# Attention with beacon tokens and a SwiGLU block on one core: all large matmuls as pairs of 64-row halves, with PSUM as four slots

## The chip, the cores and the metric

The kernel runs on one core of one Trainium2 chip. The metric is the device time of one execution in microseconds (us), as the median of several runs. Profiles and traces come from one profiled execution.

## What is computed

Eight batches of eight heads, 576 tokens each, 64 values per head. 16 beacon keys and values stand ahead of each head's own ones; every query sees them, and the rest is causal. The attention's output, 4608 tokens of 512 values, goes through a SwiGLU block.

```python
k_all = np.concatenate([beacon_k, k], axis=2)        # 16 + 576 keys
scores = scale * np.matmul(q, k_all.transpose(0, 1, 3, 2))
scores = np.where(causal, -1e9, scores)              # beacons are always seen
a = np.exp(scores - scores.max(-1, keepdims=True))
a /= a.sum(-1, keepdims=True) + 1e-09
x = np.matmul(a, v_all)                              # 8 x 8 x 576 x 64 -> 4608 x 512
g = x @ w_gate                                       # 512 x 1536
out = (g / (1 + np.exp(-g)) * (x @ w_val)) @ w_out   # 1536 x 512
```

All inputs and the output are float32; the kernel computes its matmuls in bf16 and accumulates in float32.

## The kernel before

**Order of the work.** The schedule is written out by hand: a long string, the plan, holds one letter for each piece of work, and `piece` issues the instructions of that letter on their engines. Each engine works through its own instructions in that order and waits where data or a buffer are missing. The letters that matter here: `s`, `d`, `e` are a unit of scores (masked on TensorE, on DVE, on POOL; up to three of them make a burst), `P` is the product of one head's weights with its values (pv), `G` is a unit of gate and value (512 tokens by 128 of the 1536 columns), `F` is one matmul of the output projection, `U` transposes keys and queries of a pair of heads, `X` transposes attention output, `t` is a DMA transpose, `l`, `w`, `o` are loads.

**Attention.** A pair of heads has four units of scores, A to D, with 496, 464, 336+80+80 and 208 query columns. In `scores` (line 291) each matmul contracts the 64 values of one head: the even head of a pair lies on partitions 0 to 63, the odd one on 64 to 127. So the score matmuls use 64 of the array's 128 rows, and the two heads' matmuls follow each other, each into its own PSUM bank. `exponent` (line 261) applies exp on ACT, and masks by POOL (line 269) or DVE (line 265); a few units are masked by a matmul (`mask_on_pe`, line 250). `pv` (line 315) multiplies a head's 128 key rows by 65 columns (64 values and a one, whose product is the softmax's sum), 15 matmuls a head, and DVE normalizes (lines 323, 324).

**Keys and queries.** Those of batch 0 are loaded in runs of six neighbouring rows, regrouped and transposed on TensorE (`transpose_pair`); those of batches 1 and 2 are loaded row by row and transposed on TensorE (`transpose_both`, line 229), those of later batches by DMA (`dma_transposes`). All loads of POOL's queue are issued by POOL and cast to bf16 on the way.

**The block behind.** `gv_mm` (line 360) puts gate and value of a unit into the two banks of one tile: four matmuls with 128 rows and 512 columns for each. `gv_act` takes them through tanh on ACT (line 373) and two DVE operations (lines 375, 378) into `hT`. `out_steps` (line 399) adds twelve matmuls of 128 rows and 512 columns into one bank for 128 tokens; DVE copies the result (line 408) and SP's queue stores it.

**PSUM** has eight banks: three double ones in the pool `big` (scores, gate and value, the transposes of batches 1 and 2), one in `att` (pv) and one in `outp` (projection); small work alternates between the last two (`small`).

Of the kernel before, what the change touches and what calls it, by code (L numbers as in the profile page):

```python
# [14 lines left out]
P = 128  # L15
S = 576
D = 64
# [7 lines left out]

NPE = 3

NPEX = 1

ROWS = 6  # L30
RP = S // ROWS

NHT = 2

NPT = 3

SPLIT = 4

QBLOCKS = [(0, 112), (112, 128), (240, 128), (368, 128), (496, 80)]

# [11 lines left out]
def p_col(t, q):  # L52

    if t == 0 and q >= 496:
        return 1296 + q - 496
    return q + (0, 496 - 112, 960 - 240, 1456 - 368, 1376 - 496)[t]
# [3 lines left out]
def kernel(  # L60
# [21 lines left out]
    NPAIR = H // 2  # L82
    assert NCH == B + 1 and B > NPE
# [8 lines left out]
    big = ctx.enter_context(tc.tile_pool(name="big", bufs=3, space=bass.MemoryType.PSUM))  # L92
    att = ctx.enter_context(tc.tile_pool(name="att", bufs=1, space=bass.MemoryType.PSUM))
    outp = ctx.enter_context(tc.tile_pool(name="outp", bufs=1, space=bass.MemoryType.PSUM))

    ctx.enter_context(tc.manual_schedule())

    ident = static.tile([P, P], BF16, name="ident")
    below = static.tile([P, P], BF16, name="below")
    upper = static.tile([P, P + NB], BF16, name="upper")  # L100


    QK = NKT * H * D
    QKP = ROWS * H * D
    beacons = static.tile([NB, H, D], BF16, name="beacons")
    beacons_in = static.tile([NB, H, D], FP32, name="beacons_in")
    qs = static.tile([P, QKP], BF16, name="qs")
    ks = static.tile([P, QKP], BF16, name="ks")
    first_k = static.tile([RP, 2 * ROWS * D], FP32, name="first_k")
    first_q = static.tile([RP, 2 * ROWS * D], FP32, name="first_q")  # L110
    qb = [static.tile([P, n], BF16, name=f"qb{i}") for i, n in ((0, QKP), (1, QK))]
    kb = [static.tile([P, n], BF16, name=f"kb{i}") for i, n in ((0, QKP), (1, QK))]
# [10 lines left out]
    def tiles(t):  # L123
        return t[:, 0:QK].rearrange("p (c h d) -> p c h d", c=NKT, d=D)

    def load_runs(t, src, h0, h1):
        nc.gpsimd.dma_start(  # L127
            t[0:RP, ROWS * D * h0 : ROWS * D * h1].rearrange("p (h e) -> p h e", e=ROWS * D),
            src[0, h0:h1].rearrange("h (p i) d -> p h (i d)", i=ROWS),
        )  # L130

    heat = []
    loaded = {}

    def rows(eng, dst, src, b, h0, h1, c, p0, r, n):
        key = (b, "v") if src is v or src is beacon_v else (b, src is not q, c)
        loaded[key] = loaded.get(key, 0) + 1
        return eng.dma_start(  # L138
            dst[p0 : p0 + n, c, h0:h1, 0:D], src[b, h0:h1, r : r + n, :].rearrange("h j d -> j h d")
        )  # L140

    def q_loads(b, h0, h1):
        d = tiles(qb[b % 2])
        return [
            lambda c=c, n=n: rows(nc.gpsimd, d, q, b, h0, h1, c, 0, P * c, n)
            for c, n in enumerate((P, P, P, P, 64))
        ]

    def key_loads(eng, d, src, bsrc, b, h0, h1):
        loads = [  # L150
            lambda: rows(eng, d, bsrc, b, h0, h1, 0, 0, 0, NB),
            lambda: rows(eng, d, src, b, h0, h1, 0, NB, 0, P - NB),
        ]
        for c, n in ((1, P), (2, P), (3, P), (4, 80)):
            loads.append(lambda c=c, n=n: rows(eng, d, src, b, h0, h1, c, 0, P * c - NB, n))
        return loads

    def k_loads(b, h0, h1):
        return key_loads(nc.gpsimd, tiles(kb[b % 2]), k, beacon_k, b, h0, h1)

    def v_loads(b, h0, h1):
        return key_loads(nc.gpsimd, vb[b % 2], v, beacon_v, b, h0, h1)
# [10 lines left out]
    def load_wo(i):  # L173
        fs = slice(6 * i, 6 * i + 6)
        nc.gpsimd.dma_start(  # L175
            wo[:, fs, :], moe_w_out.rearrange("(f p) e -> p f e", p=P)[:, fs, :]
        )


    def parts_of(eng):  # L180
        return ((nc.vector, 0, SPLIT), (nc.scalar, SPLIT, ROWS)) if eng is None else ((eng, 0, ROWS),)

    def regroup(dst, src, m, eng):
        cols = slice(2 * ROWS * D * m, 2 * ROWS * D * (m + 1))
        to = dst[0:RP, cols].rearrange("p (i h d) -> p i h d", i=ROWS, h=2)
        of = src[0:RP, cols].rearrange("p (h i d) -> p i h d", i=ROWS, h=2)
        for e, i0, i1 in parts_of(eng):
            copy(e, to[:, i0:i1], of[:, i0:i1])
# [7 lines left out]
    def transpose_pair(dst, src, n, m, pool, tag, eng):  # L196
        t_ps = pool.tile([P, KPAD], BF16, name="t_ps", tag=tag)
        h = slice(2 * m, 2 * m + 2)

        first = n - 64  # L200
        if first:
            nc.tensor.transpose(t_ps[:, 0:NB], beacons[:, h, :], ident[0:NB, 0:NB])
        for i in range(ROWS):
            col = P * (ROWS * m + i)
            nc.tensor.transpose(
                t_ps[:, NB + RP * i : NB + RP * i + RP], src[0][0:RP, col : col + P], ident[0:RP, 0:RP]
            )
        if first:
            copy(eng or nc.vector, dst[0][:, m, 0:NB], t_ps[:, 0:NB])
        to = dst[0][:, m, first : first + S].rearrange("q (p i) -> q p i", i=ROWS)  # L210
        of = t_ps[:, NB : NB + S].rearrange("q (i p) -> q p i", i=ROWS)
        for e, i0, i1 in parts_of(eng):
            copy(e, to[:, :, i0:i1], of[:, :, i0:i1])

    def transpose_k(m, pool, tag, eng=None):
        transpose_pair(kT, kb, 80, m, pool, tag, eng)

    def transpose_q(m, pool, tag, eng=None):
        transpose_pair(qT, qb, 64, m, pool, tag, eng)

    def transpose_both(b, m, engines):

        t_ps = big.tile([P, 2, 1024], BF16, name="t2_ps", tag="big")
        h = slice(2 * m, 2 * m + 2)
        for i, src in ((0, kb), (1, qb)):
            t = tiles(src[b % 2])
            for c in range(NKT):
                r = P if c < 4 else 80 if src is kb else 64
                nc.tensor.transpose(t_ps[:, i, P * c : P * c + r], t[0:r, c, h, :], ident[0:r, 0:r])  # L229
        for i, dst, n, eng in ((0, kT, NB + S, engines[0]), (1, qT, S, engines[1])):  # L230
            copy(eng, dst[b % 2][:, m, 0:n], t_ps[:, i, 0:n])

    def dma_transposes(b):
        def one(dst, src, c, n):
            assert loaded[b, src is kb, c] == (2 if src is kb and c == 0 else 1)
            nc.sync.dma_start_transpose(
                dst[b % 2][:, :, P * c : P * c + n],
                src[b % 2][0:n, H * D * c : H * D * c + H * D],
            )

        todo = []
        for c in range(NKT):
            todo.append(lambda c=c: one(kT, kb, c, P if c < 4 else 80))
            todo.append(lambda c=c: one(qT, qb, c, P if c < 4 else 64))
        return todo

    def mask_on_pe(u, ps):
        for hh in range(2):
            for col, n, d in UNITS[u][3]:
                nc.tensor.matmul(  # L250
                    ps[:, hh, col : col + n],
                    lhsT=below[:],
                    rhs=ident[:, d : d + n],
                    start=False,
                    stop=(col, n, d) == UNITS[u][3][-1],
                )

    def exponent(b, m, u, mask, ps):
        c0, w, _, diagonals = UNITS[u]
        p = pt[(NPAIR * b + m) % NPT]  # L260
        nc.scalar.activation(p[:, :, c0 : c0 + w], ps[:, :, 0:w], ACT.Exp, scale=0.125)  # L261
        for col, n, d in [] if mask == "s" else diagonals:
            ap = p[:, :, c0 + col : c0 + col + n]
            if mask == "d":
                nc.vector.tensor_tensor(  # L265
                    out=ap, in0=ap, in1=upper[:, None, d : d + n].to_broadcast([P, 2, n]), op=ALU.mult
                )
                continue
            nc.gpsimd.affine_select(  # L269
                out=ap,  # L270
                in_=ap,
                compare_op=ALU.is_ge,
                fill=0.0,
                base=d,
                pattern=[[0, 2], [1, n]],
                channel_multiplier=-1,
            )

    def scores(burst):

        tiles = [big.tile([P, 2, 512], FP32, name="s_ps", tag="big") for _ in burst]
        while heat:
            heat.pop()
            nc.tensor.matmul(
                tiles[0][:, 0, 0 : 2 * P], lhsT=pt[2][:, 0, 0:P], rhs=pt[2][:, 0, 0 : 2 * P], start=True, stop=True
            )
        for (b, m, u, mask), ps in zip(burst, tiles):
# [10 lines left out]
            if mask != "s":  # L298
                exponent(b, m, u, mask, ps)
# [193 lines left out]

# [162 lines left out]
```

The softmax here doesn't subtract the row's maximum and nothing guards it: scores larger than these inputs give would overflow.

## Time and profile before

| | |
|---|---|
| time, three runs | 370.61 us (median), 370.41 to 372.05 |
| profiled execution, first to last instruction (span) | 370.0 us |
| what lies around the span, median less span | 0.6 us |
| TensorE, VectorE (DVE), ScalarE (ACT), GpSimd (POOL) busy | 98%, 66%, 46%, 39% |
| granted TensorE clock, mean | 0.999 |
| DMA packets | 160,978, of which 149,040 under 512 bytes |

How to read the lines: a group's line gives the source line, the engine, the operation with what it writes and reads, the array's rows*columns, the shape and the count; behind the bar stand the time covered, the mean ns of one, and the idle time before them with what ended it. Matmuls are pipelined, so one begins before the one ahead has ended; where they follow each other closely, the distance of their starts is their price, not their duration. PE is TensorE's matmuls, PEld its weight loads. The timeline's rows give start, duration, and how many equal instructions are merged into the row.

### The profile page before, as it was taken

What the parts mean: (1) busy time and instruction counts of PE and PEld (TensorE: products, weight loads), DVE (VectorE), ACT (ScalarE), POOL (GpSimd) and SP (SyncE); (2) the same over time, 40 slices, a digit from 0 to 9 for tenths busy, and PEclk for the clock granted to TensorE, in tenths of its full rate; (3) what the DMA queues carried; (4) which work ended last, traced back from release to release, by engine and by line L of the source; (5) the groups of instructions that cost most, each with busy time, mean ns of one, the idle gap of its engine ahead of it and who ended that gap; (6) DMA issues with size and microseconds to landing.
All of it is one profiled execution on the core that took longest, in us unless ns stands there. A gap on an engine that the chain in (4) does not pass through costs nothing.

```text
span 370.0 us, 7297 instructions
## 1 busy us (share of the span) xinstructions
PE 360.8 (98%) x2851; PEld 179.3 (48%) x2851; DVE 242.8 (66%) x485; ACT 170.8 (46%) x246; POOL 143.7 (39%) x235
## 2 busy tenths in 40 slices
PE   7898989999999999999999999999999999999996
PEld 3653455655445555444455454544554444444443
DVE  4848767768827677576666765758476856655652
ACT  5933376853482567464554356254642312212110
POOL 8975569696199563726236014030200000000000
PEclk9999999999999999999999999999999999999999
DMA  9999999999999999989939859455102100001013
GB/s 165 139 191 179 191 166 149 137 168 140 173 113 197 130 135 140 166 112 112 185 54 108 77 114 86 67 61 98 59 31 41 51 30 28 30 29 57 2 59 111
DMA packets 160978, 39.61 MB, mean 107 GB/s; under 512 B 149040, under 2 KB 156464, under 8 KB 160944
## 3 DMA queue, kind: packets, MB, share of 16 engines
q0 software_dynamic: 112304, 18.83, 72.0%
q1 hardware_dynamic: 48432, 20.02, 27.7%
q8 instruction: 22, 0.36, 0.4%
q10 hardware_dynamic: 208, 0.29, 0.3%
q14 instruction: 12, 0.10, 0.1%
HBM read 38.27 MB, written 9.44 MB: 129 GB/s over the span
## 4 chain that ended last, share of the span: by engine, by line
PE 84%; POOL 7%; DMA 7%; DVE 1%; issue 1%; ACT 0%; POOLq 0%
PE gv_ps L360 45%; PE o_ps L399 25%; PE pv_ps L315 7%; PE s_ps L291 6%; DMA kb<-in_k_dram 3%; DMA vb<-in_v_dram 3%; POOL vb L138 2%; POOL kb L138 1%; PE t_ps L229 1%; POOL wg L167 1%; POOL p L269 1%; PE o_ps L419 1%; POOL wv L167 1%; POOL wo L175 0%; POOL qs L127 0%
## 5 line engine op out<-in xcount | busy, mean ns | idle before, releaser
L373 ACT ACTIVATE th<-gv_ps 128x512 f32<-128x512 f32 x108 | 64.4, 597 | 157.7 <-PE gv_ps L360 152.6
L375 DVE SCALAR_TENSOR_TENSOR u<-th,gv_ps 128x512 f32<-128x512 f32 x108 | 74.2, 687 | 63.5 <-ACT th L373 62.2
L360 PE MATMUL gv_ps<-xT,wg 128*128 128x512 bf16 x432 | 111.8, 379 | 1.3 <-DVE hT L378 1.3
L360 PE MATMUL gv_ps<-xT,wv 128*128 128x512 bf16 x432 | 111.8, 379 | 0.2 <-DMA wv<-in_moe_w_val_dram 0.2
L261 ACT ACTIVATE p<-s_ps 128x992 bf16<-128x992 f32 (+2 forms) x128 | 101.6, 869 | 21.8 <-PE s_ps L291 19.5
L399 PE MATMUL o_ps<-wo,hT 128*128 128x512 bf16 x420 | 110.1, 380 | 0.1
L378 DVE SCALAR_TENSOR_TENSOR hT<-gv_ps,u 128x512 bf16<-128x512 f32 x108 | 74.7, 691 | 3.7
L269 POOL TENSOR_SCALAR_AFFINE_SELECT p<-p 128x256 bf16<-128x256 bf16 (+2 forms) x86 | 32.8, 407 | 111.0 <-ACT p L261 108.4
L360 PEld LDWEIGHTS <-wv 128*128 128x128 bf16 x432 | 42.2, 98 | 51.3 <-DMA wv<-in_moe_w_val_dram 0.7
L360 PEld LDWEIGHTS <-wg 128*128 128x128 bf16 x432 | 41.0, 98 | 47.3 <-issue 1.5
L399 PEld LDWEIGHTS <-hT 128*128 128x128 bf16 x420 | 36.9, 98 | 42.4 <-issue 5.9
L315 PEld LDWEIGHTS <-p 128*128 128x128 bf16 x960 | 36.5, 97 | 14.6 <-issue 2.7
L315 PE MATMUL pv_ps<-vb,p 128*128 128x65 bf16 x960 | 40.1, 193 | 1.3 <-DMA vb<-in_v_dram 0.9
L265 DVE TENSOR_TENSOR p<-p,upper 128x256 bf16<-128x256 bf16 (+2 forms) x60 | 16.6, 300 | 29.2 <-ACT p L261 28.9
L138 POOL DMA_DIRECT2D vb<-in_v_dram x40 | 34.1, 865 | 3.7 <-DMA kb<-in_k_dram 2.3
L291 PE MATMUL s_ps<-qT,kT 64*128 64x80 bf16 (+4 forms) x384 | 33.1, 281 | 0.8 <-ACT p L261 0.7
L138 POOL DMA_DIRECT2D qb<-in_q_dram x35 | 30.4, 869 | 7.1 <-DVE p L265 3.1
L324 DVE TENSOR_TENSOR x<-pv_ps,rec 128x320 bf16<-128x320 f32 x64 | 31.5, 492 | 2.3
L138 POOL DMA_DIRECT2D kb<-in_k_dram x35 | 30.5, 871 | 3.4 <-DMA wo<-in_moe_w_out_dram 3.1
L408 DVE COPY o_sb<-o_ps 128x512 f32<-128x512 f32 x35 | 23.9, 684 | 7.3 <-PE o_ps L399 7.2
L291 PEld LDWEIGHTS <-kT 64*128 64x128 bf16 x384 | 13.8, 94 | 21.0 <-issue 16.3
L323 DVE RECIPROCAL rec<-pv_ps 128x5 f32<-128x5 f32 x64 | 12.0, 188 | 11.2 <-PE pv_ps L315 10.9
(57 smaller groups left out, 83.8 us busy)
## 6 DMA issues: line engine op xcount, KB each, us to landing
out_dram<-o_sb SPq DMA_DIRECT2D x35, 256.0 KB, 2.3
qb<-in_q_dram POOLq DMA_DIRECT2D x28, 128.0 KB, 6.5
vb<-in_v_dram POOLq DMA_DIRECT2D x24, 128.0 KB, 5.4
kb<-in_k_dram POOLq DMA_DIRECT2D x21, 128.0 KB, 6.6
wg<-in_moe_w_gate_dram POOLq DMA_DIRECT2D x4, 384.0 KB, 9.8
wv<-in_moe_w_val_dram POOLq DMA_DIRECT2D x4, 384.0 KB, 8.7
wo<-in_moe_w_out_dram POOLq DMA_DIRECT2D x2, 768.0 KB, 11.0
vb<-in_v_dram POOLq DMA_DIRECT2D x8, 112.0 KB, 4.8
```

Of the source, the lines that this page charges most:

```text
L138: return eng.dma_start(dst[p0 : p0 + n, c, h0:h1, 0:D], src[b, h0:h1, r : r + n, :].rearrange("h j d -> j h d"))
L261: nc.scalar.activation(p[:, :, c0 : c0 + w], ps[:, :, 0:w], ACT.Exp, scale=0.125)
L269: nc.gpsimd.affine_select(out=ap, in_=ap, compare_op=ALU.is_ge, fill=0.0, base=d, pattern=[[0, 2], [1, n]], channel_multiplier=-1,)
L291: nc.tensor.matmul(ps[:, hh, col : col + n], lhsT=kT[b % 2][r, m, P * t : P * t + P], rhs=qT[b % 2][r, m, q0 : q0 + n], start=mask != "s" ...
L315: nc.tensor.matmul(o_ps[:, c, 0 : D + 1], lhsT=pt[(NPAIR * b + m) % NPT][:, hh, col : col + P], rhs=vb[b % 2][:, t, h, 0 : D + 1], start=( ...
L324: nc.vector.tensor_tensor(out=xs[b][:, :, D * h : D * h + D], in0=o_ps[:, :, 0:D], in1=rec[:].to_broadcast([P, NKT, D]), op=ALU.mult,)
L360: nc.tensor.matmul(gvs[f][:, TOK * half : TOK * half + TOK], lhsT=w[:, kk, P * f : P * f + P], rhs=xT[:, kk, r : r + TOK], start=(kk == 0) ...
L373: nc.scalar.activation(th[:], ps[:, 0:TOK], ACT.Tanh, scale=0.5)
L375: nc.vector.scalar_tensor_tensor(out=u[:], in0=th[:], scalar=1.0, in1=ps[:, 0:TOK], op0=ALU.add, op1=ALU.mult)
L378: nc.vector.scalar_tensor_tensor(out=hTs[j][:, f, :], in0=ps[:, TOK:1024], scalar=0.5, in1=u[:], op0=ALU.mult, op1=ALU.mult)
L399: nc.tensor.matmul(st["o"][:], lhsT=hTs[j][:, f, P * i : P * i + P], rhs=wo[:, f, :], start=(f == 0), stop=(f == NF - 1),)
L408: nc.vector.tensor_copy(o_sb[:], st["o"][:])
```

## The change

Every large matmul is cut along its contraction into two halves of 64 rows. One half contracts partitions 0 to 63, the other 64 to 127, and the two of a pair write two banks of one PSUM tile. In the first phase the lower half works on the first bank's sum (gate, or the first 128 tokens, or the first head) while the upper half works on the second bank's (value, the next 128 tokens, the second head). In the second phase they swap, so that each bank gets the other 64 rows. Between the phases of one tile, `halves` issues a nop on TensorE that waits for the last matmul of that tile's first phase. Transposes of keys and queries and the masks on TensorE are in 64-row halves too; the transposes of attention output in batch 0 (`x_turn`) stay at 128 rows.

All PSUM work takes one of four double banks (`take`, `give`), the one that has been free longest by the work list's order. pv and its normalization take two heads at once, the projection two blocks of 128 tokens. Keys and queries of batches 0 to 2 are loaded in runs of nine rows (keys on the lower 64 partitions, queries on the upper) and regrouped and turned on TensorE; so there are 118 loads in place of 135, and the weights stand earlier in POOL's queue. Exp, masks, tanh and the DVE steps have letters of their own in the work list, 23 of the output copies are on DVE and 15 on ACT, and 79 masks are on DVE and 67 on POOL.

The diff, cut to its core:

```diff
-NPEX = 1
-ROWS = 6
+HALF = 64
+ROWS = S // HALF
+NSLOT = 4
...
+    def take(key, shape, dtype, name):
+        i = spare.pop(0)
+        held[key] = i
+        t = slots[i].tile(shape, dtype, name=name, tag="slot")
+        for bank in range(2):
+            writers.pop((i, bank), None)
+        return t
+
+    def give(key):
+        spare.append(held.pop(key))
+
+    def halves(key, bank, row, o, l, r, start, stop, turn=False):
+        at = (held[key], bank)
+        was = writers.get(at)
+        if was is not None and was[0] != row:
+            last = max((w for (i, _), w in writers.items() if i == at[0]), key=lambda w: w[2])
+            if last[3]:
+                gate = nc.tensor.nop()
+                tc.add_manual_dep(
+                    gate.ins,
+                    last[1],
+                    mybir.DependencyInfo(mybir.DependencyClass.Sync, mybir.DependencyReason.DATA),
+                    reason="one bank, two row halves",
+                )
+            for other, w in writers.items():
+                if other[0] == at[0]:
+                    writers[other] = (w[0], w[1], w[2], False)
...
+            ins = nc.tensor.matmul(o, lhsT=l, rhs=r, start=start, stop=stop)
+        order[0] += 1
+        writers[at] = (row, ins.ins.name, order[0], True)
...
+    def turn(n):
...
+        for i in range(ROWS):
+            for row in range(2):
+                r = slice(HALF * row, HALF * row + HALF)
+                halves(("t", n), row, row, t_ps[:, row, HALF * i : HALF * i + HALF], g[r, i, :], ident[r, r], 1, 1, True)
...
+    def pv(n, second):
+        b, m = divmod(n, NPAIR)
+        if not second:
+            pvs[n] = take(("p", n), [P, 2, 512], FP32, "pv_ps")
+        o_ps = pvs[n]
         for c, (q0, _) in enumerate(QBLOCKS):
             for t in range(c + 1):
                 col = p_col(t, q0)
...
+                for row in (1, 0) if second else (0, 1):
+                    hh = row ^ second
+                    r = slice(HALF * row, HALF * row + HALF)
+                    halves(
+                        ("p", n), hh, row, o_ps[:, hh, 68 * c : 68 * c + D + 1],
+                        pt[n % NPT][r, hh, col : col + P], vb[b % 2][r, t, 2 * m + hh, 0 : D + 1],
+                        c == 0 and t == 0 and not second, second and c == t == NKT - 1,
+                    )
...
+        for second, kk in steps:
+            for row in (1, 0) if second else (0, 1):
+                half = row ^ second
+                k64 = slice(HALF * row, HALF * row + HALF)
+                halves(
+                    ("g", n), half, row, ps[:, half, :],
+                    (wg, wv)[half][k64, kk, P * f : P * f + P], xT[k64, kk, r : r + TOK],
+                    half not in seen, final and (second, kk) == steps[-1],
                 )
...
+            second, f = divmod(st, NF)
+            for row in (1, 0) if second else (0, 1):
+                bank = row ^ second
+                k64 = slice(HALF * row, HALF * row + HALF)
+                halves(
+                    key, bank, row, projected[pr, part][:, bank, cols],
+                    hTs[j][k64, f, P * (i + bank) : P * (i + bank) + P], wo[k64, f, cols],
+                    st == 0, st == 2 * NF - 1,
                 )
...
+        elif kind == "G":
+            gate_value(n + wholes, [(0, kk) for kk in range(KD)], False)
+        elif kind == "H":
+            gate_value(n + wholes, [(1, kk) for kk in range(KD)], True)
...
+        "2Ha1Ga2G1H2Ga1H2Ga1H2Ha1FaFFF2FFG12GHHa1Ga2FFF1G2FFFHGa1H2Ha1Ga2FFF1G2FFFFFFFFFFoFFFoFFFFFFFFHHa",
```

In the new work list `S` or `s` is a unit of scores, `E` its exp, `D` or `M` its masks, `P` and `p` are the two phases of pv, `R` the normalization, `G` and `H` the two phases of gate and value, `a`, `1`, `2` the steps from them to `hT`, `F` one pair of the projection, `O` and `o` the output copies, `T` a turn of keys and queries.

## The prediction

> **What bounds the kernel now.** The page comes first: its busy shares, and the chain that ended last.
>
> ```profile
> PE 360.8 (98%) x2851; PEld 179.3 (48%) x2851; DVE 242.8 (66%) x485; ACT 170.8 (46%) x246; POOL 143.7 (39%) x235
> ...
> PE 84%; POOL 7%; DMA 7%; DVE 1%; issue 1%; ACT 0%; POOLq 0%
> ```
>
> TensorE has work all the time, and no other engine is near it; the 14% of POOL and DMA in the chain lie before 53 us. A busy TensorE may still be held up, so I asked the groups by shape and then the timeline of one stretch.
>
> ```profile
> L360 PE MATMUL gv_ps<-xT,wv 128*128 128x512 bf16 x432 | 111.8, 379 | 0.2 <-DMA wv<-in_moe_w_val_dram 0.2
> L399 PE MATMUL o_ps<-wo,hT 128*128 128x512 bf16 x420 | 110.1, 380 | 0.1
> L315 PE MATMUL pv_ps<-vb,p 128*128 128x65 bf16 x960 | 40.1, 193 | 1.3 <-DMA vb<-in_v_dram 0.9 <-DVE x L324 0.2
> L291 PE MATMUL s_ps<-qT,kT 64*128 64x496 bf16 x64 | 12.1, 374 | 0.1
> ```
>
> A matmul of 512 columns shows 379 ns from first to last, but they start 216 ns apart. The 64 score matmuls of 496 columns cover 12.1 us, which is 32 times 378 ns: the two halves (rows 0 to 63, rows 64 to 127) of a pair run at once.
>
> ```profile
> 160.17 1.03 PE L360 MATMUL gv_ps<-xT,wv 128*128 128x512 bf16 x4
> 161.13 0.58 PE L291 MATMUL s_ps<-qT,kT 64*128 64x496 bf16 x4
> 161.64 0.82 PE L399 MATMUL o_ps<-wo,hT 128*128 128x512 bf16 x3
> 162.30 0.62 PE L315 MATMUL pv_ps<-vb,p 128*128 128x65 bf16 x15
> 162.76 0.81 PE L399 MATMUL o_ps<-wo,hT 128*128 128x512 bf16 x3
> 163.50 0.69 PE L291 MATMUL s_ps<-qT,kT 64*128 64x336 bf16 x10
> 164.12 0.39 PE L399 MATMUL o_ps<-wo,hT 128*128 128x512 bf16 x1
> ```
>
> Each row's start plus its matmuls times their pitch should be the next row's start. 160.17 + 4 x 0.216 = 161.03, but the scores start at 161.13. Their pairs of 496 and 464 columns stream 0.40 us, to 161.53, but the projection starts at 161.64. 162.30 to 162.76 is 15 x 0.030, with nothing lost. So about 0.1 us goes wherever 128-row and 64-row work meet, and nowhere else. Taking every start in the trace less columns/2.4 + 2.5 ns: 115 such meetings lose 95.7 ns each (11.0 us), 6 around the 16-row beacon transposes lose 0.65 us, and the first matmul or pair behind a meeting takes 10 ns more (226 instead of 216), 1.15 us: 12.8 us in all.
>
> ```profile
> PEld L291 <- issue: 16.3, 39, 0.6
> ...
> PE gv_ps L360 <- DVE hT L378: 1.3, 1, 1.3
> ...
> PE pv_ps L315 <- DMA vb<-in_v_dram: 0.9, 2, 0.5
> PE s_ps L291 <- ACT p L261: 0.7, 2, 0.4
> ```
>
> The waits say the same: weights for scores stand idle at 39 places for nothing the profile shows. Real waits behind the first transpose add up to 7.1 us, all but 0.2 before 61 us.
>
> The sum of the span of 370.0 us: first real matmul 6.0; streaming 341.2 (gate and value 186.5, projection 93.2, pv 28.4, scores with masks 26.0, transposes 7.2); meetings and their followers 12.2 (net of some 0.6 where pairs start early); waits 7.1; tail 3.3. The three runs have a median of 370.6, so 0.6 lies around the span.
>
> **The change, part by part.**
>
> *Every large matmul as two 64-row halves: -11.9 us.* With all work in 64-row halves the meetings go: -12.8. The four transposes of x in batch 0 (x_turn) stay at 128 rows, 8 meetings x 0.106 = +0.85. Price of a pair: in the scores, behind the first pair of a burst, pairs follow each other after columns/2.4 + 2 to 3 ns (80 to 80 columns, 31 of 31; 336 to 80, 16 of 16), the next weights loading 8 to 10 ns after the current pair starts. 512/2.4 + 2.5 = 216, what a 128-row matmul takes now. So 1296 pairs of the MLP cost the same: 0, with a bound of +10 ns each (the first pair's excess), +13.0.
>
> The Trainium skill speaks against this: "TensorE: Matmul & The Clock Gate", section "Wait — 56ns, not 53.3ns?", has matmuls start at least 25 ns apart however small. By that figure a pv pair would take 50 ns instead of 29, an estimate of +20 us over 960 pairs, and the gain would be gone. The trace's halves start 3 to 4 ns apart, so I go by the trace.
>
> *pv: +1.5 us (0 to +9.3).* The 960 matmuls of 128x65 become 960 pairs for two heads at once. Nearest rows: 29 ns for one of 65 columns, 35 for a pair of 80. New is the number of instructions, four in 29 ns. From an empty queue (a semaphore instruction at 221.73) to the next such one at 222.16, TensorE's sequencer passed 40 instructions in 0.387 us, 9.7 ns each; by that a pair takes 39 ns, 10 x 960 = 9.3 us if the sequencer never runs ahead. The trace has it up to 33 instructions ahead, over half of one phase's 60. I take 1.5.
>
> *The swap: +3.0 us (2.7 to 4.6).* Between a slot's first and second phase `halves` puts a nop that waits for the slot's last matmul; behind it queues all further TensorE work, and through it the exp, tanh and copies. From the end of streaming: 379 - 216 = 163 ns until the matmul ends, 14 to the semaphore's event, 43 to a start (the medians of TensorE's waits); or, where a sequencer instruction (51 ns) waits, 57 more behind it: 230 to 330 ns. I went through the new work list and added up the streaming between each slot's last first-phase matmul and its gate: of 162 gates, 112 have over 450 ns, 33 have 250 to 450 (mostly 425 to 444, two projection steps), 7 have 89 to 214 and 10 have none (five in the first 13 us of this streaming, two by 41, three in the last projections). 10 x 0.23 to 0.33, 7 x about 0.06 to 0.16 and a few tens of ns for six of 254 to 311: 2.7 to 4.6; part of the early ones lie under waits for data.
>
> *Keys and queries of batches 1 and 2 by runs: -2.7 us on TensorE.* 132 transposes (6.2 us) become 12 turns of 9 pairs of 64 columns, 29 ns each, and 12 for beacons: 3.5. If the pairs ran one half after the other it would be 6.7, +0.5. Beside it, off the path: 22 row loads on POOL (0.55 to 0.87 us each) become 5 loads at 0.65 to 0.74, so POOL's queue gets some 15 us shorter; eight more regroupings on DVE, 8 x 0.75 (the 96x768 copy at 0.50, times 1.5) = 6 us; the copies to kT and qT stay near 0.53 to 0.74 each. DVE's normalization falls from 64 x 0.68 to 32 x at most 1.17 us. DVE keeps about a third idle, so this is nothing; without that cover the 6 us would be the price.
>
> *Masks on TensorE: -0.6 us.* 28 matmuls of 80 to 128 columns (1.4 us) become 28 pairs of up to 64 (0.8). POOL's masks fall from 86 to 67, DVE's rise from 60 to 79, 19 x 0.3 = 5.7 us under DVE's idle time. Exp and tanh are unchanged; 15 output copies move to ACT, 15 x 0.6 = 9 us, into its 54% of idle time.
>
> *Four slots and the new order: +1.0 us (-3 to +6).* pv and the projection each had a bank of their own; now each takes one of four two-bank slots, which leaves two or three for scores or gate and value. The late MLP stage fits: a gate-value unit holds a slot for 1.73 us of matmuls and 0.60 + 0.69 + 0.69 + some 0.1 of ACT and DVE, 3.8 us in all; three slots would turn one over every 1.3 us, and TensorE needs 1.73. In the attention stage two slots for scores turn over in 0.2 + 1.0 (exp) each. Weights come earlier and batch 1's keys cost fewer packets, so the early waits of 7.1 may shrink by 3 or, the order being new, grow; I leave them and put 1.0 for slots.
>
> Sum: 370.0 - 11.9 - 2.7 - 0.6 + 1.5 + 3.0 + 1.0 = 360.3, and 0.6 around it: 360.9 us.
>
> **The rivals.**
>
> *Slots run short (slower).* With the projection and pv each holding a slot, a score unit must wait for an exp to release one. Place: each of the 32 pairs of heads, from 50 to 280 us. Price: one exp (1.0 us) less the first pv phase (0.45) that covers it, 0.55 x 32 = 17.6: 378 us. It cancels the gain from 0.30 us a pair on and makes it slower from 0.36. For it: scores now wait only 0.7 us in all because three double banks serve them. Against: ACT is 46% busy, and a burst's exp has other work behind it.
>
> *Pairs and instructions cost their upper bounds in part.* Half of pv's 9.3 and 3 ns on each of 1296 pairs: 4.7 + 3.9 - 1.5 = +7.1: 368 us. For it: instructions on TensorE nearly double, and every gate takes away the sequencer's lead. Against: the 31 of 31.
>
> *The meetings don't go; a swap is one.* Swapping halves drains the array as a change of shape does: 162 x 0.106 = 17.2: 378 us. Against: halves alternate in the scores at 3 ns with no loss; only accumulation into one bank from both halves is new.
>
> **How the numbers follow.** Forecast 0.68, with its own range 355 to 366 (upper: gates 4.6, pv 5, slots 2; lower: waits 3 less, pv and slots 0). Slots 0.15, upper bounds 0.13, swap as a meeting 0.04. About 0.5% (1.9 us) can be told from no change. Faster: 0.68 + 0.08 of the second rival = 0.76; same: 0.04 of it and 0.02 of the first = 0.06; slower: 0.13 + 0.01 + 0.04 = 0.18. The range 355 to 373 leaves out 0.06 below and some 0.14 above.
>
> **What would show it.** Right: gate and value matmuls in two halves 3 to 4 ns apart, pairs at 216 ns; no 0.1 us between scores and their neighbours; pv pairs at 29 to 35 ns; TensorE starts at most 0.33 us late at a swap, and only where nothing lies between. Wrong: pairs at 226 or more, pv pairs near 39 or 58, waits of scores for an exp of several us in all, or waits behind 61 us.

## The result and the profile after

After: 425.87 us (median, 424.41 to 429.09); before, on the same chip: 370.83 us (370.41 to 372.05). The ratio is 1.149 (95% interval 1.143 to 1.154): 15% slower, where 360.9 us with a range of 355 to 373 had been predicted. The profiled execution of after has a span of 424.1 us. Further down, runs over 1.5% above the fastest of their kernel (two of one_gate's four, one of filled's six) are left out of times and ratios as slow.

The page of after first: shares of the span, granted clock in 40 slices, a queue of instruction fetches (number, MB, share of the DMA engines), and the chain that ended last.

```profile
PE 391.4 (92%) x5263; PEld 186.5 (44%) x5263; DVE 233.6 (55%) x424; ACT 184.6 (44%) x266; POOL 123.0 (29%) x200
PEclk9777959999999999999999999999999999999999
q8 instruction: 41, 0.67, 0.7%
PE 83%; DMA 9%; POOL 3%; issue 2%; ACT 1%; DVE 0%; ACTq 0%
```

TensorE fell from 98% to 92% busy although its busy time grew by 30.6 us: it is held up in the middle of its work. The granted clock shows sevens and a five in the first 64 us, where it was at half for 27 us. No other engine came nearer to the bound. TensorE's timeline shows one unit of gate and value (start, duration, instructions):

```profile
355.28 0.38 PE L132 MATMUL gv_ps<-xT,wv 64*128 64x512 bf16 x1
355.49 0.38 PE L132 MATMUL gv_ps<-xT,wg 64*128 64x512 bf16 x1
355.50 0.38 PE L132 MATMUL gv_ps<-xT,wv 64*128 64x512 bf16 x1
355.71 0.38 PE L132 MATMUL gv_ps<-xT,wg 64*128 64x512 bf16 x2
356.16 0.39 PE L132 MATMUL gv_ps<-xT,wv 64*128 64x512 bf16 x1
356.17 0.39 PE L132 MATMUL gv_ps<-xT,wg 64*128 64x512 bf16 x1
356.39 0.38 PE L132 MATMUL gv_ps<-xT,wv 64*128 64x512 bf16 x1
```

Until 355.71 a pair starts every 0.216 us, its halves some 4 ns apart, as predicted. One of the two `wg` at 355.71 opens a unit's second phase, behind the gate; it starts 3 ns after its neighbour, so this gate cost nothing. The `wv` that should come with it or 0.216 us later starts at 356.16: for 0.45 us no matmul starts. The waits of the weight loads show how often (total, times, longest):

```profile
PEld L132 <- PE gv_ps L132: 63.4, 121, 0.6
PEld L132 <- PE o_ps L132: 10.5, 25, 0.6
PEld L132 <- POOL p L329: 10.2, 2, 9.8
PEld L132 <- PE pv_ps L132: 9.3, 28, 0.6
```

TensorE waits for itself 174 times: about the 162 swaps, not the ten at which nothing lies between. (Weight loads run ahead, so these times overlap the matmuls; the standstills of the array itself are shorter, see the table.) The third row is nearly all one wait of 9.8 us for a mask of POOL.

To see the parts, I let every matmul stream its columns at the granted clock from its recorded start and sorted what is left of each span: *work* (streaming at full clock), standstills of the array by length, *one half* (one half of the rows streaming alone, half of that time), *clock* (lost to half clock, that is a granted clock of 0.5; ahead of the clock's first record the first matmuls start 0.427 us apart, so half clock is taken there). In us:

| kernel | span | work | 60-150 ns | 150-350 ns | over 700 ns | other idle | one half | clock |
|---|---|---|---|---|---|---|---|---|
| before | 370.0 | 335.4 | 12.4 | 1.9 | 6.9 | 11.3 | 0.7 | 1.5 |
| after | 424.1 | 331.4 | 1.3 | 42.1 | 19.4 | 5.0 | 15.6 | 9.2 |
| masks_only | 415.2 | 331.4 | 1.6 | 41.8 | 9.1 | 5.2 | 16.1 | 10.0 |
| one_gate | 392.4 | 331.4 | 1.8 | 3.5 | 34.6 | 3.9 | 7.5 | 9.7 |
| one_gate_masks | 390.6 | 331.4 | 1.3 | 4.1 | 32.2 | 4.3 | 7.5 | 9.8 |
| data_on_time | 373.3 | 331.4 | 1.5 | 3.5 | 15.8 | 5.3 | 7.2 | 8.6 |
| pv_whole | 375.7 | 331.4 | 12.3 | 3.0 | 11.0 | 7.8 | 4.6 | 5.6 |
| filled | 371.2 | 331.4 | 1.3 | 4.4 | 14.1 | 6.9 | 6.6 | 6.5 |

The meetings (60 to 150 ns) went, as they should: 12.4 to 1.3. In their place came 178 standstills of 0.24 us, longer waits, and half clock.

### The profile page after: what moved, and what is told of

The parts are those of the page before. It is cut to its first block, busy times and chain, and to the rows that moved or that the text cites. A ratio compares the mean times of both kernels' runs of the same rounds, so it can differ in the third digit from the quotient of the medians.

```text
span 424.1 us, 12037 instructions
## 1 busy us (share of the span) xinstructions
PE 391.4 (92%) x5263; PEld 186.5 (44%) x5263; DVE 233.6 (55%) x424; ACT 184.6 (44%) x266; POOL 123.0 (29%) x200
## 4 chain that ended last, share of the span: by engine, by line
PE 83%; DMA 9%; POOL 3%; issue 2%; ACT 1%; DVE 0%; ACTq 0%
PE gv_ps L132 47%; PE o_ps L132 24%; PE pv_ps L132 8%; DMA qk<-in_q_dram 4%; PE s_ps L132 4%; DMA wv<-in_moe_w_val_dram 4%; DMA first<-in_k_dram 1%; POOL p L329 1%; ACT p L316 1%; POOL qk L169 1%; POOL qk L160 0%; PE t_ps L130 0%; POOL wg L200 0%; POOL wv L200 0%; POOL wo L208 0%
## 5 line engine op out<-in xcount | busy, mean ns | idle before, releaser
L132 PE MATMUL gv_ps<-xT,wg 64*128 64x512 bf16 x864 | 218.1, 381 | 0.6 <-ACT p L316 0.2
L132 PE MATMUL gv_ps<-xT,wv 64*128 64x512 bf16 x864 | 200.8, 381 | 8.2
L132 PE MATMUL o_ps<-wo,hT 64*128 64x512 bf16 (+2 forms) x912 | 126.4, 365 | 1.5
L132 PEld LDWEIGHTS <-wv 64*128 64x128 bf16 x864 | 67.3, 94 | 87.8 <-PE gv_ps L132 58.1
L132 PEld LDWEIGHTS <-wg 64*128 64x128 bf16 x864 | 68.7, 94 | 48.5 <-PE gv_ps L132 3.0
L132 PEld LDWEIGHTS <-hT 64*128 64x128 bf16 x912 | 49.9, 94 | 41.9 <-PE o_ps L132 10.2
L132 PE MATMUL pv_ps<-vb,p 64*128 64x65 bf16 x1920 | 50.1, 192 | 13.9 <-POOL p L329 9.9
L132 PEld LDWEIGHTS <-p 64*128 64x128 bf16 x1920 | 40.0, 95 | 29.9 <-POOL p L329 10.2
L361 DVE TENSOR_TENSOR x<-pv_ps,rec 128x640 bf16<-128x640 f32 x32 | 26.4, 824 | 1.2
L169 POOL DMA_DIRECT2D qk<-in_q_dram x25 | 21.5, 860 | 12.0 <-DMA qT<-qk 9.4
## 6 DMA issues: line engine op xcount, KB each, us to landing
wv<-in_moe_w_val_dram POOLq DMA_DIRECT2D x4, 384.0 KB, 10.8
wo<-in_moe_w_out_dram POOLq DMA_DIRECT2D x2, 768.0 KB, 12.4
```

The source lines that it names most:

```text
L132: ins = nc.tensor.matmul(o, lhsT=l, rhs=r, start=start, stop=stop)
L169: return nc.gpsimd.dma_start(dst[p0 : p0 + n, c, :, 0:D], src[b, :, r : r + n, :].rearrange("h j d -> j h d"))
L361: nc.vector.tensor_tensor(out=xs[b][:, :, P * m : P * m + P].rearrange("p c (h d) -> p h c d", d=D), in0=o[:, :, :, 0:D], in1=rec[:].to_br ...
```

## The experiments

**The theory.** Reading `halves` again after the result: the gate sets the flags of a slot to False, but the matmul behind it records itself with True. The next matmul, on the other bank and the other rows, finds the slot's latest writer to be *that* matmul, flagged True, and issues a second gate, which waits for the matmul just issued. Nothing can lie between. So the theory (A) is a second gate at each of 162 swaps. Its rivals: swapping halves costs this by itself (B), or the gate that is left is hidden only in part (C).

**one_gate: the second gate taken out.** It asks whether the entry that the new matmul replaces was still ungated; the first gate already waits for every matmul of the first phase.

```diff
-            if last[3]:
+            if was[3]:
```

> Only the second gate of each swap is taken away (the one that waits for the swap's own first matmul). Theory A: that second gate is what costs; 162 swaps lose 0.234 us of standstill, 0.010 for the pair behind it and about 0.1 for the half that streams alone, 55 us together; a span of about 369 us against 424. Rival B: the swap itself drains the array, whatever the number of gates, since the first gate stays: over 415 us. Rival C: the single gate is hidden only in part (0.1 us each): about 385.

Measured: 396.5 us (two runs, 394.1 and 398.9), ratio 1.069 (1.061 to 1.077). TensorE's waits for itself, 174 in after, are down to 15:

```profile
PEld L132 <- PE gv_ps L132: 3.8, 8, 1.0
PEld L132 <- PE o_ps L132: 2.1, 5, 0.6
PEld L132 <- PE pv_ps L132: 0.3, 2, 0.2
```

The standstills of 150 to 350 ns fell from 42.1 to 3.5 us and *one half* from 15.6 to 7.5: 46.7 us, or 0.29 us a swap, so A holds, and B and C fall: 3.5 us is close to the 1.9 of before. But the time fell by 29 us (the span by 31.7) and not by the 55 forecast: standstills over 0.7 us grew from 19.4 to 34.6. The gates had hidden other waits, which none of the three names.

**drain_before: the price of such a gate, in the kernel before.** Each of the 108 gate-and-value units gets one nop behind its first value matmul, waiting for it.

```diff
+                if half == 1 and kk == 0:
+                    gate = nc.tensor.nop()
+                    tc.add_manual_dep(gate.ins, mm.ins.name, ...)
```

> The kernel before, with one nop in each of its 108 gate-value units that waits for the matmul just issued, as the second gate of a swap does. Theory A: each lets the array stand 0.234 us and delays the next matmul by 0.010: 108 x 0.244 = 26 us more, 397. Rival: without halves the queue hides part of it: under 385.

Measured: 395.99 us, ratio 1.067 (1.063 to 1.071); (396.0 - 371.1) / 108 = 0.23 us each. The waits show them, all but one:

```profile
PEld L360 <- PE gv_ps L360: 58.8, 107, 0.6
```

The price is the same with 128 rows as with the 64 of after (0.24 us). After's 0.29 has also the half that streams alone.

**masks_only and one_gate_masks: the long wait for POOL.** POOL's timeline in after (start, duration, instruction, idle before and what ended it):

```profile
47.03 0.89 POOL L169 DMA_DIRECT2D vb<-in_v_dram  x1 [2.63 <-PE s_ps L132]
51.95 0.73 POOL L169 DMA_DIRECT2D vb<-in_v_dram  x1 [4.04 <-DMA wo<-in_moe_w_out_dram]
54.47 0.53 POOL L169 DMA_DIRECT2D qk<-in_beacon_k_dram  x1 [1.78 <-DMA qk<-in_k_dram]
57.53 0.83 POOL L169 DMA_DIRECT2D qk<-in_k_dram  x1 [2.54 <-DMA qk<-in_q_dram]
...
60.11 1.06 POOL L329 TENSOR_SCALAR_AFFINE_SELECT p<-p 128x256 bf16<-128x256 bf16 x3
```

Loads of later batches wait for earlier transfers (4.04, 1.78, 2.54 us); masks that pv needs from 50.8 us on stand behind them in POOL's order and run at 60.11. The two kernels give the masks of six units (the forecasts say five) to DVE (`M` to `D` in the work list), one with both gates, one with the first alone.

> Both gates of each swap stay; only the masks of five units of batch 1 move from POOL to DVE. If the standstill at 51 us is POOL's queue: 414 us, 10 less than 424. If it is the data: 424.

> The same with the masks of five units of batch 1 moved from POOL to DVE, so that pv no longer waits behind POOL's loads. Theory A and the 9.8 us standstill before pv at 51 us as a cost of its own: about 360 us, near the forecast. Rival: something else (a load, exp) keeps that pv waiting, so no more than 2 us below the kernel with one gate alone.

Measured: masks_only 416.76 us (1.124; 1.121 to 1.127), one_gate_masks 392.24 us (1.056; 1.050 to 1.063). With both gates the long wait goes and the time falls by 9, about as expected. With one gate it falls by 4 (the span by 1.8), to 392 and not to the 360 forecast: a wait for masks stays. Taking the second gate out is worth 24.5 us here (416.76 - 392.24), as against 29 without the masks moved; 46.3 us of standstills and half-empty array go, and 23.1 us come back in standstills over 0.7 us. The waits of one_gate_masks name them:

```profile
PE gv_ps L132 <- DMA xT<-x: 7.3, 3, 3.5
PE pv_ps L132 <- POOL p L329: 7.2, 1, 7.2
PE pv_ps L132 <- issue: 5.0, 4, 1.8
PE gv_ps L132 <- issue: 1.8, 1, 1.8
```

One more mask behind loads; three waits for the DMA transposes of attention output into `xT`, which a slower TensorE had hidden; and pauses in which TensorE waited for nothing that the profile shows, as in this piece of the chain of one_gate_masks:

```profile
115.49 0.39 PE pv_ps L132 x26
115.87 1.76 issue
117.63 0.24 PE pv_ps L132 x4
```

A fetch of 16 KB of instructions begins at 114.94 in the trace, 2.7 us before TensorE goes on. Five such pauses (7.7 us) end 2.4 to 3.0 us after the start of a fetch; the kernel before has none, with 22 fetches against 41. After and masks_only, which are slower, have the same 41 and no such pause behind the first 30 us.

**whole_mlp: 64-row halves for attention alone.** One_gate_masks with gate, value and projection at 128 rows.

```diff
-            for row in (1, 0) if second else (0, 1):
-                halves(("g", n), half, row, ps[:, half, :], (wg, wv)[half][k64, ...], xT[k64, ...], ...)
+            nc.tensor.matmul(ps[:, second, :], lhsT=(wg, wv)[second][:, ...], rhs=xT[:, ...], ...)
```

> One gate and moved masks as before, and the MLP's matmuls whole again (128 rows, gate's four and then value's four in the same places of the work list); scores, pv and turns stay in halves. By the price of a meeting of 64- and 128-row work (0.106 us), the work list has 283 of them instead of 8: 275 x 0.106 = 29 us more than with halves, less up to 3 us of gates of the MLP: about 387 us. If halves cost the MLP anything per pair, less than that.

Measured: 405.15 us, ratio 1.092 (1.089 to 1.096); 13 us above one_gate_masks, not 27. The meetings are priced right: 245 standstills of 60 to 150 ns make 24.7 us, 0.101 each. What I missed is on the other side: with 31 fetches instead of 41 the pauses fall from 6.8 us in TensorE's waits to 1.2, all in the first 30 us, and the waits for `xT` from 7.3 to 3.1. The rest of the 14 us was not taken apart.

**data_on_time: masks and transposes in time.** One gate, the masks of positions 150 to 330 of the work list on DVE, and `V`, which issues the DMA transposes of a batch's attention output, directly behind the batch's last `R`.

```diff
-        "Gal1SGEl2SHlEDPaDSHE1p2aMSRGE1MH2SGaE1SHME2PaDSFpE1FFRFSFEFF2SFFFEDMFFDFcPcTcpkTQFFkFQTFFqRSFFEF",
+        "Gal1SGEl2SHlEDPaDSHE1p2aDSRGE1DH2SGaE1SHDE2PaDSFpE1FFRFSFEFF2SFFFEDDFFDFcPcTcpkTQFFkFQTFFqRVSFFE",
```

> One gate; all POOL masks up to the end of batch 1's attention on DVE; the DMA transposes of attention output issued directly behind the normalization of each batch's last heads instead of up to 22 pieces later. If pv's wait for POOL (7.3 us) and the three waits of gate and value for those transposes (7.8 us) are delays of their own: 375 us, and with the half clock that follows such a standstill 371. Rival: the waits for transposes were pauses for instructions in disguise, which stay: 383.

Measured: 375.04 us, ratio 1.011 (1.005 to 1.016), as expected for the waits; the 371 that counted on half clock going too was not reached. What still stands against it are these waits, and half clock (8.6 against 1.5 us):

```profile
PE pv_ps L132 <- issue: 4.0, 4, 1.8
PE gv_ps L132 <- DMA xT<-x: 3.4, 1, 3.4
```

**pv_whole: fewer instructions, with the meetings.** data_on_time with pv at 128 rows (a `for hh` matmul in place of the two `halves`).

> The same, with pv as whole matmuls of 128 rows, one head in each of the two places, so 1,920 fewer instructions on TensorE. If the pauses behind instruction fetches (7.7 us) come from too many short instructions in a row: they vanish, and 126 meetings of 64- and 128-row work at 0.106 us add 12.5: about 5 us more than the kernel it is made from. If those pauses are something else, they stay, and it is 12 us more.

Measured: 377.68 us, ratio 1.018 (1.014 to 1.022), 2.6 above data_on_time. 126 standstills of 60 to 150 ns make 12.3 us, 10.8 more, but after the start no pause behind a fetch is left and half clock lost 3.0 less. That the fetches *cause* the pauses is not shown; fewer instructions took them away in both kernels that had fewer.

**column_halves_before: instructions by themselves.** The kernel before, each MLP matmul as two of 256 columns.

```diff
+                for c in (0, TOK // 2):
+                        gvs[f][:, TOK * half + c : TOK * half + c + TOK // 2],
```

> The kernel before, with every matmul of the MLP as two of 256 columns behind two weight loads, all 128 rows: 2,568 more instructions on TensorE, no swap, no gate, no new work list. If the mere number of instructions at 54 ns each is free: 1,284 more starts at 2.5 ns, 3.2 us more, 373.6. If instructions run short at that number: over 380.

Measured: 374.2 us, ratio 1.008 (1.006 to 1.011): 1284 more matmuls cost 3.1 us, 2.4 ns each. Number alone, at 108 ns each, is nearly free; of the five pauses of one_gate_masks four came where instructions are shortest, in pv, and one in gate and value.

**filled, warm_start, filled_and_warm: the half clock and the last wait.** data_on_time, with twelve `F` moved ahead of the wait of 3.4 us; with 21 pieces (the forecasts say 18) of two dummy matmuls where TensorE waits for loads at the start; with both.

> Kernel: data_on_time with the twelve projection steps of batch 1 moved in front of chunk 4's first gate-and-value matmuls, and nothing else. Theory: the xT wait at 179.6 (3.58 us) falls below 1 us and no half clock follows it (182.4 to 189.2 before, 3.4 us lost): 375 - 2.6 to 3.6 - 3.4 = 368 to 369. Rival (half clock not tied to the standstill): 371 to 372, with an interval of half clock still somewhere behind 170 us. If the next chunk's transfer only comes later by as much, nothing changes: 375.

> Kernel: data_on_time with 18 pieces of two 64-row matmuls of 256 columns, whose products nobody reads, in places of the first 10 us where TensorE waits for loads, and nothing else. Theory: the half clock of 8.3 to 18.5, which follows TensorE's idle time at the start, goes; it lost up to 5 us, and some of TensorE's work there waits for loads anyway: 370 to 372. Rival (half clock at the start belongs to something other than TensorE's idle time, or waits for loads hide it): 374 to 376, and the extra matmuls cost at most 1 us.

> Kernel: data_on_time (373.3 us of span) with two edits. (1) Twelve projection steps of batch 1 are moved in the work list to just before the first gate-and-value matmuls of chunk 4, where TensorE stood 3.58 us for chunk 4's xT at 179.6. (2) 18 pieces of two 64-row matmuls of 256 columns, whose products nobody reads, are put into places of the first 10 us where TensorE waits for loads. Theory (standstills of about 2 us and more cost twice: the wait itself, and some 3.4 to 10 us of half clock behind it): the wait of 3.58 goes and with it the half clock of 182.4 to 189.2 (3.4 us lost), and the half clock of 8.3 to 18.5 (up to 5 us lost) goes too: 373.3 - 2.6 to 3.6 - 3.4 - 4 to 5 = 361 to 364 of span, 363 to 366 with what lies around it, below the kernel before (371). Rival (the half clock has its own rhythm, or the pauses behind instruction fetches move with the work and open it elsewhere): only the wait goes, 369 to 372, the same as before.

Measured: 374.13 (1.008; 1.005 to 1.010), 380.08 (1.025; 1.023 to 1.027) and 378.44 us (1.019; 1.016 to 1.023). The wait for `xT` fell from 3.4 to 1.5 us in filled, and the half clock at 182.4 to 189.2 went; but an interval of half clock came at 24.7 and a new pause of 1.0 us behind a fetch at 154, and the median moved by less than the runs' spread, not to the 368 to 369 forecast. In warm_start the half clock at 8.3 to 18.5 went, as forecast, and the kernel became 5 us slower: the dummy matmuls stream for 2.4 us, score matmuls there wait for exp (0.61 us at 14.8, 0.46 at 15.7), another interval of half clock came at 28.8, and later waits for `xT` grew to 6.2 us. My forecast of 4 to 5 us gained by a warm start was wrong, and with it the 363 to 366 of both edits; what bounds that stage was not taken apart. No version beat the kernel before.

**long_stands and short_stands: what half clock follows.** The kernel before, with six standstills of 2.74 us, or 24 of 0.92, set into gate-and-value units: a nop that waits for four additional tanh, or one.

```diff
+                    if stood[0] in (48, 58, 68, 78, 88, 98):
+                        for _ in range(4):
+                            act = nc.scalar.activation(stand[:], gvs[f][:, 0:TOK], ACT.Tanh, scale=0.5)
+                        gate = nc.tensor.nop()
+                        tc.add_manual_dep(gate.ins, act.ins.name, ...)
```

> Kernel: the kernel before, with six standstills of TensorE set in by hand in the gate-and-value units 48, 58, 68, 78, 88 and 98 of 108: behind the first value matmul a nop waits for four additional tanh (0.60 us each) into a tile that nobody reads, so TensorE stands for about 2.6 us each time, 15 to 16 us in all. Theory (a standstill of 2 us and more is followed by half clock): the profile shows intervals of half clock behind them, 3.4 us or more each, which cost another 1.7 us or more: 371 + 15.6 + 10 or more = 396 or more. Rival (half clock has its own rhythm and only met the standstills by chance): granted clock stays at 1.0 as in the kernel before, 386 to 388.

> Kernel: the kernel before, with 24 short standstills in every second gate-and-value unit from 48 to 94: the nop waits for one additional tanh, so TensorE stands for about 0.8 us, 19 us in all. Theory (the half clock follows the length of one standstill, not their sum): no half clock, granted clock 1.0, 371 + 19 = 388 to 391. Rival (it follows the idle share): half clock here too, 395 or more.

Measured: 391.77 us (1.058; 1.054 to 1.062) and 392.74 us (1.062; 1.057 to 1.066). The granted clock of long_stands, then of short_stands:

```profile
PEclk9999999999999999998999999999998998999999
```

```profile
PEclk9999999999999999999999999999999999999999
```

Three of the six long standstills are followed by 3.4 us of half clock (from 181.8, 294.5 and 321.8 us; the standstills end at 181.6, 294.4 and 320.8), three by none; none of the short ones is. 6 x 2.74 + 3 x 1.7 = 21.5, measured 21.1; 24 x 0.92 = 22.1, measured 22.0. So half clock does follow single long standstills, but not each, and not the sum of idle time. In one_gate it followed one of 2.1 us (ended at 123.2, half clock from 123.8); two of 1.9 to 2.0 us in one_gate_masks were followed by none. My forecast for long_stands took it for each and was 4 us too high. The Trainium skill ("TensorE: Matmul & The Clock Gate", section "HAM oscillation — how this bites in real kernels") warns of idle gaps over about 3.4 us; here 2.74 us were enough in half of the cases.

## Why the prediction was wrong

**The step that failed: "The swap: +3.0 us (2.7 to 4.6)".** It counted one gate a swap, "112 have over 450 ns" of other work between, and priced ten gates. The section on the change says one nop, too. The code issues two, and the second has nothing between at any of the 162. At 0.29 us each, which is inside the 0.23 to 0.33 that the step itself gave to a gate with nothing between, that is 46.7 us, on top of the first gates, which were forecast at 3.0 and cost some 1.6 (3.5 us of standstills in one_gate against 1.9 before). The price was right, the number of gates wrong, by a misreading of one line (`last[3]` taken for the flag of the replaced entry). The corrected sum is 360.9 - 3.0 + 1.6 + 46.7 = 406.2, and the rival "a swap is a meeting" was wrong too: a swap without that gate adds almost no standstill (one_gate: 15 standstills of 150 to 350 ns in all, 8 before).

**The second failure: "Four slots and the new order: +1.0".** The slots are right: scores wait for exp 0.6 us in after, and the rival's 17.6 are not there. The order is wrong, and its bound of +6 too: it left the early waits as they were. 9.9 us of waits for masks behind loads in POOL's queue, and 7.7 us more of half clock than before, make up most of the other 20 us; which part of the half clock the new order brought is not shown. I had noted that POOL's queue gets shorter, but not what its masks stand behind. With one gate the same step hides 15 us more, as longer waits for masks, waits for `xT` and pauses behind fetches, which no term of the sum held.

**What was right.** Meetings: -11.9 forecast, -11.1 measured, and +10.8 where pv_whole brings 126 of them back. Pairs: 216 ns. pv: +1.5 forecast; a pair takes 29 to 31 ns (30 matmuls in 0.45 to 0.46 us in the chain of data_on_time), where the floor that the prediction weighed would have made 50. Turns and masks: -3.3 forecast, *work* fell by 4.0. Two 64-row halves have a small cost that I had at 0: in data_on_time "one half" is 6.5 above the kernel before, but "other idle" 6.0 below, so it is near 0 after all.

So with one gate and data in time the change is worth what its parts promised, 11 + 4 us, and loses it again to half clock (7) and to waits for data and pauses behind fetches (9; over 0.7 us: 15.8 against 6.9): 375.0 against 371.1.

## What to carry to other kernels

Count waits from the instruction stream that the code emits, case by case, and not from what its author's helper means to emit: one flag that a matmul sets again doubled the gates and cost 47 us. A wait of TensorE for its own latest matmul let the array stand for 0.23 to 0.24 us here, with 65 as with 512 columns and with 64 as with 128 rows; the gates with half a microsecond of other work ahead of them cost nothing. When a stall is taken from the bound engine, look for what was late just behind it (here masks behind loads, transposes, instruction fetches): only 24 to 32 of the 47 us came back until those were moved.

## What the runs showed of the hardware

- Work of 64 and of 128 rows in turn costs 0.10 us a meeting (245 standstills in whole_mlp, 126 in pv_whole); two 64-row halves swapping banks add almost no standstill (15 of 150 to 350 ns in one_gate with 162 swaps, 8 in before).
- After a standstill of 2.74 us TensorE had half clock for 3.4 us in three cases of six; after 0.92 us, never in 24.
- In the kernels with one gate and 41 fetches of 16 KB of instructions (22 in before), TensorE pauses 0.7 to 2.2 us, mostly in pv's short matmuls, and in one_gate_masks 2.4 to 3.0 us after the start of a fetch. The slower kernels with both gates have 41 fetches too and no such pause behind the first 30 us, nor have those with 31 to 34. Whether the fetch itself is the cause stays open.
- Masks of POOL that pv needed stood behind POOL's own loads, which by the profile waited for earlier transfers (up to 4.0 us each): TensorE waited 9.7 us for them in after, 13.1 in one_gate.
